# Gathers behind a branch, loads behind a gather, an earlier w_in, and a new set of aims in a fused attention, expert and MLP kernel

## The chip, the cores and the metric

The kernel runs on one core of one Trainium2 chip. The metric is the device time of one execution in microseconds (us), lower is better. The engines are PE (matmul), DVE (VectorE), ACT (ScalarE), POOL (GpSimd) and SP, which issues most transfers; POOL issues the indirect ones. Each engine takes its instructions in order.

## The reference

Three stages follow each other. x is [4, 576, 512].

```python
# 1: attention, 4 batches x 8 heads, seq 576, head_dim 64
scores = q @ k.T / sqrt(64)
keep = scores >= max(scores) - tau            # tau = 0.02, the rest is masked out
x = softmax(scores where keep) @ v            # heads side by side: [4, 576, 512]

# 2: one of 8 experts for each token, with a sticky choice along the sequence
logits = x @ w_gate;  gate = sigmoid(x @ w_local)
e[s] = argmax(logits[s]) if s == 0 or gate[s] < 0.5 else e[s-1]
x = softmax(logits)[e] * (relu(x @ w1[e]) @ w2[e])       # w1: 512x1024, w2: 1024x512

# 3: gated MLP over tokens
h = gelu_tanh(x @ w_in);  u, v = h[:512], h[512:]
vn = layernorm(v) * g_ln
out = x + (u * (w_sg @ vn + b_sg)) @ w_out               # w_sg mixes the 576 positions
```

## The kernel before

**One list.** Every operation of the kernel is put into one graph with an engine, a planned duration and an aim (a due time), and a list scheduler turns it into five queues, one per engine. `Graph.order` picks by aim, and the operations run in the order that it chose. The recorded operations are issued from one helper, so in the profile most of the later stages carry the line L183. Attention's aims come from `Attn.build` with tables (`OFFS`, `PER` and the letters in `KE`, `QE`, `KL`, `QL`, `NB`), the later ones from `Tail.P` and `PRIO`. An aim decides only the place in a queue; the hardware waits by semaphores.

**Attention.** 144 row tiles (128 rows x 576 columns) go through scores (L427), row maximum on DVE (L432), the negated maximum (`nb`: ACT L440 or POOL L442), exponential on ACT (L447), mask and sum on DVE (L456), transposes (L476) and the product with v (L515, L517). Each of the 32 head and batch pairs has its q and k split into a high part (rounded copy, on ACT L380 or DVE L382) and a low part (the remainder, L395 for k and L406 for q, on DVE or POOL). The letters of the tables name the engine for each: A, D or P.

**Routing.** `Route` works in two halves of the tokens and a rest. A half is some thirty small operations on DVE and a few on PE. Half A ends in L1123 on DVE and L1128 on PE; it says which expert is first (`oe`), so that its weights can be loaded and its first two tiles gathered before attention is over. The rest gives the permutation `inv` for all tokens (rank counts, L1210 on PE), from which every tile of 128 tokens is gathered out of `x_dram` by POOL.

**Experts.** 22 tiles in the order of the experts, with the capacities CAPS = (5, 3, 3, 3, 2, 2, 2, 2). The first expert's first two tiles run in `plain` in full float32; its other three, and all tiles of the experts 1 to 7, run as three products of high and low parts. The weights of an expert are eight loads of 512 KB (`wld`), taken into a ring of six buffers (c_75 to c_80), split by ACT (high) and DVE (low). Expert 0 is followed by a branch (`over`, L1697) for tiles that overflow the capacities; it isn't taken here, but every engine reads a register and jumps at that place. The aim of the branch is `more` in `Tail.P`.

```python
g.gather(need - a * P["gth"], gth, w=[xg], deps=dep["A"] if t < 2 else dep["R"], name="gth")   # L1386
W8.append(split(*load(i, k, need, st, [dep["rank"]]), need, self.WLO[i]))                      # L1479
```

**Conversions and MLP.** Beside the experts' work twelve conversions (`cv`: three steps on DVE, three on POOL, one on DVE) rewrite `w_in` and `w_out` into `wi` and `wo` in device memory. The MLP takes its rows in groups of three tiles. Its four slices of `w_in` are loaded from `wi` into the same ring and split: high parts on ACT, low parts (`two`, 128x1024) in turn on POOL and DVE. The first group's tiles are gathered by POOL from `ys`, where the experts stored their rows; PE holds 30 bf16 matmuls without a use (`idle`) ahead of the first transposes.

## Time and profile before

| what | us |
|---|---|
| median of three runs (797.89 to 801.44) | 799.79 |
| the profiled execution | 798.59 |
| its span | 796.8 |
| PE busy in it | 764.4 |
| DVE busy in it | 580.7 |
| ACT busy in it | 461.6 |
| POOL busy in it | 268.5 |

The profile is one execution. The span is the time from its first to its last instruction; 1.8 us of the execution lie outside it. PE's busy time is that of its matmuls, and idle time is put down to the operation whose end came last before PE went on. "PEq" there is PE's own sequencer, and "issue" is time in which the profile shows nothing that was waited for. The mean granted clock of PE is 0.998 of full speed over the execution.

### The profile page before, as it was taken

How to read it: one execution, taken by the hardware profiler on the slowest of the kernel's cores; microseconds unless marked ns; L12 is line 12 of the kernel's file. 1: busy time of each engine (PE TensorE's matmuls, PEld its weight loads, DVE VectorE, ACT ScalarE, POOL GpSimd, SP SyncE). 2: the span in 40 equal slices, each digit the busy share in tenths (PEclk: the TensorE clock that was granted, in tenths of full speed). 3: DMA queues.
4: the chain of work that ended last, by engine and by line, in shares of the span. 5: the costliest groups of instructions: out<-in, count | busy, mean ns of one | idle time of the engine just before them, and what ended most of it. 6: DMA issues, size and time to landing. Idle time of an engine off the chain costs nothing.

```text
span 796.8 us, 13834 instructions
## 1 busy us (share of the span) xinstructions
PE 764.4 (96%) x4832; PEld 653.0 (82%) x4832; DVE 580.7 (73%) x1226; ACT 461.6 (58%) x860; POOL 268.5 (34%) x411
## 2 busy tenths in 40 slices
PE   7999999999979999799999999999999999999997
PEld 4787788888857876488898889989788999899996
DVE  7998999999999966465766667774379743587632
ACT  6888788889868864263444345543386532366410
POOL 6335143333333100312544232253675233111410
PEclk9999999999999999999999999999999999999999
DMA  7342323453253024768485576754440012300012
GB/s 211 101 151 74 110 86 126 157 175 124 61 197 117 2 80 146 227 225 278 163 275 203 179 247 223 236 194 159 146 142 0 1 53 93 84 11 1 14 41 66
DMA packets 46912, 103.18 MB, mean 129 GB/s; under 512 B 7538, under 2 KB 7538, under 8 KB 46834
## 3 DMA queue, kind: packets, MB, share of 16 engines
q1 hardware_dynamic: 43634, 91.72, 34.9%
q0 software_dynamic: 3200, 10.49, 4.5%
q8 instruction: 40, 0.66, 0.3%
q14 instruction: 38, 0.31, 0.1%
HBM read 80.17 MB, written 22.02 MB: 128 GB/s over the span
## 4 chain that ended last, share of the span: by engine, by line
PE 48%; DVE 4%; POOL 2%; DMA 2%; issue 1%; ACT 1%; SPq 0%; POOLq 0%; DVEq 0%; ACTq 0%
PE PS L183 48%; DVE MF L183 2%; POOL MF L183 1%; DVE r L183 1%; POOL r L183 1%; DMA MF<-in_w_in_dram 1%; DMA wi<-MF 1%; DMA MF<-ys,MF 1%; ACT MF L183 1%; DVE bs L183 0%; ACT r L183 0%; DVE rq L183 0%; SPq L183 0%; DVE mv L183 0%; PE PS L1251 0%
## 5 line engine op out<-in xcount | busy, mean ns | idle before, releaser
L183 PE MATMUL PS<-r,r 128*128 128x512 f32 (+3 forms) x1512 | 294.2, 352 | 2.2 <-DVE r L183 1.6
L183 PEld LDWEIGHTS PS<-r,r 128*128 128x128 f32 x1512 | 254.9, 189 | 34.1 <-DVE r L183 3.4
L427 PE MATMUL PS<-MR 128*128 128x288 f32 x640 | 122.2, 319 | 7.9 <-DVE MF L456 6.0
L456 DVE SCALAR_TENSOR_TENSOR MF<-PS,MF 128x576 f32<-128x576 f32 x144 | 116.2, 810 | 8.2 <-ACT MF L447 5.6
L447 ACT ACTIVATE MF<-PS,MF 128x576 f32<-128x576 f32 x144 | 107.0, 749 | 10.6 <-DVE MF L432 9.2
L432 DVE TENSOR_REDUCE MF<-PS 128x1 f32<-128x576 f32 x144 | 106.6, 751 | 7.2 <-PE PS L427 6.2
L427 PEld LDWEIGHTS PS<-MR 128*128 128x128 f32 x640 | 91.6, 189 | 17.3 <-DVE MF L456 10.3
L183 PE MATMUL PS<-MR,r 128*128 128x256 f32 (+2 forms) x616 | 101.7, 322 | 0.0
L183 ACT ACTIVATE r<-PS 128x512 fp32r<-128x512 f32 (+4 forms) x102 | 46.3, 472 | 94.5 <-PE PS L183 89.0
L183 PEld LDWEIGHTS PS<-MR,r 128*128 128x128 f32 x616 | 91.6, 188 | 8.1
L369 ACT ACTIVATE c<-PS 128x512 f32<-128x512 f32 (+1 forms) x160 | 84.7, 566 | 20.5 <-PE PS L476 15.2
L476 PE MATMUL PS<-ident,MF 128*128 128x128 f32 x576 | 84.2, 275 | 3.3 <-ACT c L503 1.9
L476 PEld LDWEIGHTS PS<-ident,MF 128*128 128x128 f32 x576 | 67.3, 140 | 8.1 <-ACT c L369 3.0
L183 ACT ACTIVATE MF<-PS 128x512 f32<-128x512 f32 (+1 forms) x64 | 35.6, 555 | 65.9 <-PE PS L183 50.9
L442 POOL TENSOR_TENSOR MF<-MF,cf 128x1 f32<-128x1 f32 x104 | 23.3, 225 | 138.7 <-DVE MF L432 110.6
L183 DVE TENSOR_TENSOR r<-c,r 128x1024 fp32r<-128x1024 f32 x42 | 52.0, 1265 | 22.3 <-ACT r L183 21.9
L183 DVE SCALAR_TENSOR_TENSOR MF<-MF,PS 128x384 f32<-128x384 f32 (+1 forms) x84 | 49.9, 606 | 20.8 <-ACT MF L183 20.0
L183 DVE SCALAR_TENSOR_TENSOR r<-PS,r 128x384 fp32r<-128x384 f32 (+3 forms) x64 | 29.1, 455 | 47.4 <-ACT r L183 47.3
L183 POOL TENSOR_SCALAR MF<-MF 128x512 f32<-128x512 int32 x12 | 21.9, 1825 | 102.6 <-DVE MF L183 62.1
L183 ACT ACTIVATE r<-c 128x1024 fp32r<-128x1024 f32 x46 | 46.8, 1056 | 11.1 <-PE PS L183 5.8
L183 PE MATMUL PS<-r,MR 128*128 128x320 f32 (+2 forms) x288 | 44.6, 315 | 5.4 <-PEq L1697 4.1
L183 PEld LDWEIGHTS PS<-r,MR 128*128 128x128 f32 x288 | 43.5, 195 | 6.6 <-DVEq L1697 4.3
(233 smaller groups left out, 1053.1 us busy)
## 6 DMA issues: line engine op xcount, KB each, us to landing
c<-in_w_dram SPq DMA_DIRECT2D x64, 512.0 KB, 4.5
c<-in_kP_dram SPq DMA_DIRECT2D x32, 288.0 KB, 3.5
c<-in_qP_dram SPq DMA_DIRECT2D x32, 288.0 KB, 3.1
ys<-MF SPq DMA_DIRECT2D x36, 256.0 KB, 4.3
x_dram<-c SPq DMA_DIRECT2D x6, 768.0 KB
MF<-in_w_in_dram SPq DMA_DIRECT2D x8, 512.0 KB
c<-in_vP_dram SPq DMA_DIRECT2D x12, 320.0 KB, 5.4
out_dram<-MF SPq DMA_DIRECT2D x12, 256.0 KB, 2.0
```

Of the source, the lines that this page charges most:

```text
L183: return lambda *a, **k: x(*[v(y) for y in a], **{n: v(y) for n, y in k.items()})
L369: self.nc.scalar.activation(out, src, AF.Copy, **k)
L427: self.nc.tensor.matmul(self.PS[:, banks[hf], 0:288], q, k[:, 288 * hf:288 * hf + 288], start=(n == 0), stop=(n == len(ops) - 1))
L432: self.nc.vector.tensor_reduce(m, self.tl[i]["s"], axis=AX.XY, op=ALU.min)
L442: (self.nc.vector if eng == "DVE" else self.nc.gpsimd).tensor_tensor(self.nbt(i), self.tl[i]["m"], self.tp, op=ALU.add)
L447: self.nc.scalar.activation(e.rearrange("p (a b) -> p a b", a=2), t["s"], AF.Exp, bias=t["m"], scale=-1.0)
L456: self.nc.vector.scalar_tensor_tensor(w.rearrange("p (a b) -> p a b", a=2), t["s"], self.nbt(i), t["e"].rearrange("p (a b) -> p a b", a=2) ...
L476: self.nc.tensor.transpose(p[:, c, :], t["w"][:, z + c * 128:z + (c + 1) * 128], self.cst["ident"])
```

## The change

**Dependences.** Gathers of the tiles from CAPS[0] = 5 on, which belong to the experts 1 to 7, now depend on the branch (`g.more`). A new transfer of four bytes, `hold0`, reads tile 4 after its gather and writes it into a scrap word; all loads of weights of the experts 1 to 7 depend on it. The transposes of the MLP's second group for tile i wait for the matmuls `vp` of tile i of the first.

**w_in.** Its loads are aimed 16 us earlier (T - 26 in place of T - 10), its splits 14 us earlier, and all four low parts are on DVE; POOL had two of them.

**Tables.** In attention three low parts of k (`KL` places 26, 27, 31) and two of q (`QL` 17, 30) go from DVE to POOL; of the high parts one of k (`KE` 4) and three of q (`QE` 19, 23, 31) go from ACT to DVE and one of q (`QE` 15) from DVE to ACT. Of 18 tiles five gave their negated maximum to ACT and now three do, which is 16 of 144 more on POOL. `OFFS`, `PER`, `PRIO` and `Tail.P` are new.

```diff
--- before.py
+++ after.py
@@ -238,19 +238,19 @@
     XALL, X2T, RR, EP, WP, Z, SM, LOG = 24576, F, F + 1152, F + 1736, F + 2888, F + 6920, F + 8072, F + 8200
 
 
-    KE = "AAAAAAADAAADDADAAADADAAADAAAAAAA"
-    QE = "DADAAAAAAADAADADADAAADAAAAAAAAAA"
-    KL = "PPPPDPPDPDPPPPPDDPPPPPPPPPDDDPPD"
-    NB = "PAAPAPAAPPPPPPPPPP"
-    QL = "DPPDPPPPPPPPDPPPPDPPPPDDPPPPPPDP"
-    PER = 1.8433
+    KE = "AAAADAADAAADDADAAADADAAADAAAAAAA"
+    QE = "DADAAAAAAADAADAAADADADADAAAAAAAD"
+    KL = "PPPPDPPDPDPPPPPDDPPPPPPPPPPPDPPP"
+    NB = "PAPPPPPPPPPPPAAPPP"
+    QL = "DPPDPPPPPPPPDPPPPPPPPPDDPPPPPPPP"
+    PER = 1.8091
     WB = 6
     ALPHA = 0.05368
     side = ()
     extra = ()
     WARM = (9, 2, 2, 2, 2)
     WARMP = 0.0
-    OFFS = dict(c=3.643, rem=1.219, mx=-1.591, qk=-5.409, x2t=0.022, remx=-4.025, nb=-5.597, nbm=6.508, ex=-3.128, prep=-0.874, mask=0.758, av=7.252, tr=4.058, rec=2.530, ld=-39.498, post=9.454, qd=53.614)
+    OFFS = dict(c=3.372, rem=1.016, mx=-1.496, qk=-4.928, x2t=4.442, remx=-3.519, nb=-6.117, nbm=0.077, ex=-3.520, prep=-1.662, mask=1.432, av=6.737, tr=4.551, rec=2.717, ld=-36.254, post=9.490, qd=55.875)
 
 
     SEQ = [(n, t) for t in range(9) for n in range(2)]
@@ -1277,7 +1277,7 @@
     ALPHA = (0.0326, 0.03152)
     PA = 14.8
     W0, W1 = 14.8, 23.1
-    P = dict(more=1.886, wld=13.828, whi=-5.404, wlo=6.969, gth=35.799, cv=45.362, xT=18.099, s=23.033, mgth=17.296, sgl=-14.414, fin=7.434, vh=63.286, sg=26.995, wo=46.385)
+    P = dict(more=-12.300, wld=19.348, whi=-5.770, wlo=11.562, gth=36.897, cv=31.147, xT=12.357, s=25.298, mgth=16.824, sgl=-12.676, fin=9.956, vh=63.991, sg=25.660, wo=50.081)
     WLO = "DDDDDDDD"
 
     WR = tuple(33792 + 1024 * i for i in (0, 1, 2, 3, 5, 4))
@@ -1362,7 +1362,7 @@
             a = self.ALPHA[0]
             g.op("ACT", act(1024), need - a * P["whi"], lambda: nc.scalar.activation(h, raw, AF.Copy), r=[wr], w=[uh], name="whi")
             if lo == "D":
-                g.op("DVE", dve(1024), need - a * P["wlo"], lambda: nc.vector.tensor_tensor(l, raw, h.bitcast(F32), op=ALU.subtract), r=[wr, uh], w=[ul], name="wlo")
+                g.op("DVE", 1.35, need - a * P["wlo"], lambda: nc.vector.tensor_tensor(l, raw, h.bitcast(F32), op=ALU.subtract), r=[wr, uh], w=[ul], name="wlo")
             else:
                 g.op("POOL", pool(1024), need - a * P["wlo"], lambda: nc.gpsimd.tensor_tensor(l, raw, h.bitcast(F32), op=ALU.subtract), r=[wr, uh], w=[ul], name="wlo")
             return [uh, ul], h, l
@@ -1383,7 +1383,10 @@
                     nc.tensor.transpose(p.ap[:, k * 128:(k + 1) * 128], x[:, k * 128:(k + 1) * 128], ident)
 
             q = lambda: p.ap.rearrange("p (a b) -> p a b", a=4)[:, :, 0:n]
-            g.gather(need - a * P["gth"], gth, w=[xg], deps=dep["A"] if t < 2 else dep["R"], name="gth")
+            g.gather(need - a * P["gth"], gth, w=[xg], deps=dep["A"] if t < 2 else dep["R"] + ([g.more] if t >= CAPS[0] else []), name="gth")
+            if t == CAPS[0] - 1:
+
+                self.hold0 = g.op("DQ", 0.1, need - a * P["gth"], lambda: nc.sync.dma_start(out=self.scrap[0:1, 1:2], in_=x[0:1, 0:1]), r=[xg], name="hold")
             g.op("PE", 0.44, need - a * P["xT"], tr, r=[xg], pw=p, deps=deps, name="xT")
             g.op("ACT", act(512, True), need - a * 2, lambda: nc.scalar.activation(xh, q(), AF.Copy), w=[xt], pr=p, name="xh")
             if xl is not None:
@@ -1476,7 +1479,7 @@
                 W8 = []
                 for i in range(8):
                     need = W(T + 0.3 * i if i < 4 else T + L1 + 1.3 * (i - 4))
-                    W8.append(split(*load(i, k, need, st, [dep["rank"]]), need, self.WLO[i]))
+                    W8.append(split(*load(i, k, need, st, [dep["rank"], self.hold0]), need, self.WLO[i]))
             hh, hl = self.M(self.HH, [128, 8, pitch], F32R), self.M(self.HL, [128, 8, pitch], F32R)
             hu = [g.use((self.HH + pitch * m, pitch), (self.HL + pitch * m, pitch)) for m in range(8)]
             if k == 0:
@@ -1569,7 +1572,7 @@
         def two(parts, n, h, l, raw, wr, t, eng, rows=slice(0, 128)):
             u = g.use(*parts)
             g.op("ACT", act(n), t, lambda: nc.scalar.activation(h[rows], raw[rows, 0:n], AF.Copy), r=[wr], w=[u], name="shi")
-            e, d = (nc.vector, dve(n)) if eng == "DVE" else (nc.gpsimd, pool(n))
+            e, d = (nc.vector, 1.35) if eng == "DVE" else (nc.gpsimd, pool(n))
             g.op(eng, d, t, lambda: e.tensor_tensor(l[rows], raw[rows, 0:n], h[rows].bitcast(F32), op=ALU.subtract), r=[wr, u], w=[u], name="slo")
             return u
 
@@ -1582,8 +1585,8 @@
         for k in range(4):
             wr = R["wr"].new()
             raw = self.wr[wr.i]
-            g.op("DQ", 1.46, W(T - 10), lambda k=k, raw=raw: nc.sync.dma_start(out=raw, in_=w_in[k * 128:(k + 1) * 128, :]), w=[wr], deps=self.conv, name="sld")
-            self.wiu.append(two([(s[0] + 2048 * k, 2048)], 1024, self.wi[0][:, k, :], self.wi[1][:, k, :], raw, wr, W(T - 2), "DVE" if k % 2 else "POOL"))
+            g.op("DQ", 1.46, W(T - 26), lambda k=k, raw=raw: nc.sync.dma_start(out=raw, in_=w_in[k * 128:(k + 1) * 128, :]), w=[wr], deps=self.conv, name="sld")
+            self.wiu.append(two([(s[0] + 2048 * k, 2048)], 1024, self.wi[0][:, k, :], self.wi[1][:, k, :], raw, wr, W(T - 16), "DVE"))
         self.two, self.V = two, V
 
     def s_weights2(self, after):
@@ -1754,7 +1757,7 @@
         st = [dict(x2={}, v={}, u={}) for _ in range(2)]
         ones = g.op("POOL", 2.7, W(self.P["sg"]), self.v_rows, w=[g.use(*[(x, 512) for k in (8, 9) for x in A["v"][k]])], name="rows")
 
-        first = []
+        first, self.vp = [], []
 
         def gelu2(pb, n, dst, du, t):
 
@@ -1812,10 +1815,10 @@
                     o = g.op("DVE", 0.4, W(need - 4), lambda t=t, x=x: v.tensor_scalar(x, x, self.pg[p][:, t:t + 1], None, op0=ALU.mult), r=[xu], w=[xu], name="xpg")
                     if i == 2:
 
-                        self.hold = g.op("DQ", 0.1, W(need - 4), lambda x=x: nc.sync.dma_start(out=self.scrap, in_=x[0:1, 0:1]), r=[xu], name="hold")
+                        self.hold = g.op("DQ", 0.1, W(need - 4), lambda x=x: nc.sync.dma_start(out=self.scrap[0:1, 0:1], in_=x[0:1, 0:1]), r=[xu], name="hold")
                 else:
                     g.op("ACT", act(512), W(need - 4), lambda t=t, x=x: nc.scalar.activation(x, x, AF.Copy, scale=self.pg[p][:, t:t + 1]), r=[xu], w=[xu], deps=first, name="xpg")
-                g.op("PE", 0.43, W(need - 3), tr, r=[xu], deps=self.busy if p == gi == 0 else (), pw=pb, name="xT")
+                g.op("PE", 0.43, W(need - 3), tr, r=[xu], deps=self.busy if p == gi == 0 else self.vp[i:i + 1] if p == 0 and gi == 1 else (), pw=pb, name="xT")
                 g.op("ACT", act(512, True), W(need - 2.5), lambda c=c, q=q: nc.scalar.activation(self.x2h[:, :, c], q(), AF.Copy), w=[xt[i]], pr=pb, name="xh")
                 o = g.op("DVE", dve(512), W(need - 2), lambda c=c, q=q: v.tensor_tensor(self.x2l[:, :, c], q(), self.x2h[:, :, c].bitcast(F32), op=ALU.subtract), r=[xt[i]], w=[xt[i]], pr=pb, name="xl")
             if p == gi == 0:
@@ -1833,7 +1836,7 @@
                         for n, (a, b) in enumerate(((self.x2h, 0), (self.x2h, 1), (self.x2l, 0))):
                             nc.tensor.matmul(pb.ap, a[:, k, c], self.wi[b][:, k, 512:1024], start=(k == 0 and n == 0), stop=(k == 3 and n == 2))
 
-                g.op("PE", pe(512, 12), W(T[0]), mm, r=[xt[i]] + self.wiu, pw=pb, name="vp")
+                self.vp.append(g.op("PE", pe(512, 12), W(T[0]), mm, r=[xt[i]] + self.wiu, pw=pb, name="vp"))
                 T[0] += pe(512, 12)
                 v2u, bsu = R["v2"].new(), R["bs"].new()
                 v2, bs = self.v2[v2u.i], self.bs[bsu.i]
@@ -1969,7 +1972,7 @@
     STEPS = (("G", 0, 0), ("G", 0, 1), ("G", 0, 2), ("g", 0, 0), ("g", 0, 1), ("G", 1, 0), ("G", 1, 1), ("G", 1, 2), ("g", 1, 0), ("g", 1, 1), ("4", 1, 0))
 
 
-PRIO = (10.5, 8.806, 9.0)
+PRIO = (12.465, 7.256, 9.256)
 
 
 @with_exitstack
@@ -1993,7 +1996,7 @@
     x_dram = tc.dram_tile([T, D], F32, name="x_dram")
     ys = tc.dram_tile([(NT + NOV) * 128, D], F32, name="ys")
     wi32 = tc.dram_tile([D, 2 * D], F32, name="wi32")
-    scrap = tc.dram_tile([1, 1], F32, name="scrap")
+    scrap = tc.dram_tile([1, 2], F32, name="scrap")
     wo32 = tc.dram_tile([D, D], F32, name="wo32")
     nc = tc.nc
 

```

What the tables do to the queues is not to be read from the diff. Three places follow.

**The end of attention on SP.** In these rows c_72 and c_73 take q and k, c_75 to c_78 the first expert's first four loads, and x_dram is the store of attention's result. Before, on SP, with attention's last two pairs of k and q behind the first expert's loads:

```order
L183 DMA c_75<-in_w_dram 128x1024
...
L183 DMA c_76<-in_w_dram 128x1024
...
L183 DMA c_77<-in_w_dram 128x1024
...
L183 DMA c_78<-in_w_dram 128x1024
L347 DMA c_72<-in_kP_dram 128x576
...
L343 DMA c_72<-in_qP_dram 128x576
L347 DMA c_73<-in_kP_dram 128x576
...
L343 DMA c_73<-in_qP_dram 128x576
L567 DMA x_dram<-c_74 128x3x512 x3
```

In the changed program the same stretch of SP reads:

```order
L347 DMA c_72<-in_kP_dram 128x576
...
L343 DMA c_72<-in_qP_dram 128x576
L347 DMA c_73<-in_kP_dram 128x576
...
L343 DMA c_73<-in_qP_dram 128x576
...
L183 DMA c_75<-in_w_dram 128x1024
...
L183 DMA c_76<-in_w_dram 128x1024
...
L183 DMA c_77<-in_w_dram 128x1024
...
L183 DMA c_78<-in_w_dram 128x1024
L567 DMA x_dram<-c_74 128x3x512 x3
```

The first expert's loads moved behind all of attention's loads; they wait for half A of the routing, which moved with them.

**The branch on SP and POOL.** Here c_75 to c_80 take weights of expert 1, ys are stores of the first expert's rows, scrap is `hold0`, and x_dram with inv_91 are gathers of the tiles from 2 on (inv_92 are those inside the branch). SP ahead of the branch before:

```order
L183 DMA c_78<-in_w_dram 128x1024
L183 ISA
L183 DMA c_80<-in_w_dram 128x1024
L183 ISA
L183 DMA c_79<-in_w_dram 128x1024
L183 DMA ys<-MF 128x512
L183 ISA
L183 DMA c_75<-in_w_dram 128x1024
L183 DMA ys<-MF 128x512
L183 TENSOR_LOAD oi
L183 ISA x2
L1697 COMPARE_AND_BRANCH
```

SP ahead of the branch in the changed program:

```order
L183 DMA c_76<-in_w_dram 128x2x512
L183 DMA scrap<-MF 1x1
L183 DMA MF<-in_g_ln_dram 128x512
L183 TENSOR_LOAD op
...
L183 DMA c_78<-in_w_dram 128x1024
L183 DMA ys<-MF 128x512
...
L183 DMA c_80<-in_w_dram 128x1024
L183 DMA ys<-MF 128x512
L183 TENSOR_LOAD oi
...
L1700 COMPARE_AND_BRANCH
```

Of the four loads of expert 1 two moved behind the branch, and the other two stand behind `hold0` and the load of gln. POOL around the branch before, its body left out:

```order
L183 MEMSET r_3147 128x8x64 x2
L183 DMA MF<-x_dram,inv_91 128x512 x7
L183 TENSOR_LOAD oi
L1697 COMPARE_AND_BRANCH
...
L1697 UNCONDITIONAL_BRANCH
L183 DMA MF<-x_dram,inv_91 128x512 x4
```

POOL around the branch in the changed program, its body left out:

```order
L183 MEMSET r_3142 128x8x64 x2
L183 DMA MF<-x_dram,inv_91 128x512 x3
L183 TENSOR_LOAD oi
L1700 COMPARE_AND_BRANCH
...
L1700 UNCONDITIONAL_BRANCH
L183 DMA MF<-x_dram,inv_91 128x512 x8
```

Of the seven gathers ahead of the branch three are left, and eight stand directly behind it where four stood.

**The entry of the MLP on POOL and DVE.** Here r_3110 and r_3104 are the buffers of the split weights, c_75 to c_79 the loaded slices of w_in, and ys the experts' stored rows. POOL up to the first gathers of the MLP, before:

```order
L183 TENSOR_TENSOR MF<-MF 128x512 x2
L183 MEMSET r_3110 64x512
L183 MEMSET r_3110 1x512 x2
L183 MEMSET r_3110 64x512
L183 MEMSET r_3110 1x512 x2
L183 TENSOR_TENSOR r_3110<-c_79,r_3110 128x1024
L183 TENSOR_TENSOR r_3110<-c_76,r_3110 128x1024
L183 DMA MF<-ys,MF 128x512 x7
```

POOL up to the same gathers in the changed program:

```order
L183 TENSOR_TENSOR MF<-MF 128x512 x2
L183 MEMSET r_3104 64x512
L183 MEMSET r_3104 1x512 x2
L183 MEMSET r_3104 64x512
L183 MEMSET r_3104 1x512 x2
L183 DMA MF<-ys,MF 128x512 x7
```

The two low parts in front of POOL's gathers are gone. DVE there before (128x192 are evacuations of the last expert's first layer, MF 128x512 alone steps of conversions and, as the last, of the MLP's entry):

```order
L183 SCALAR_TENSOR_TENSOR r_3147<-PS,r_3147 128x192 x2
L183 SCALAR_TENSOR_TENSOR MF<-MF 128x512
L183 SCALAR_TENSOR_TENSOR r_3147<-PS,r_3147 128x192 x6
L183 TENSOR_TENSOR r_3110<-c_75,r_3110 128x1024
L183 TENSOR_TENSOR r_3110<-c_77,r_3110 128x1024
L183 TENSOR_SCALAR MF<-MF 128x512 x3
L183 TENSOR_TENSOR r_3147<-PS,r_3147 128x4x128 x3
```

DVE at the same place in the changed program:

```order
L183 SCALAR_TENSOR_TENSOR r_3142<-PS,r_3142 128x192
L183 SCALAR_TENSOR_TENSOR MF<-MF 128x512
L183 SCALAR_TENSOR_TENSOR r_3142<-PS,r_3142 128x192 x6
L183 TENSOR_TENSOR r_3104<-c_79,r_3104 128x1024
L183 SCALAR_TENSOR_TENSOR r_3142<-PS,r_3142 128x192
L183 TENSOR_TENSOR r_3104<-c_75,r_3104 128x1024
L183 TENSOR_TENSOR r_3104<-c_76,r_3104 128x1024
L183 TENSOR_TENSOR r_3104<-c_77,r_3104 128x1024
L183 TENSOR_SCALAR MF<-MF 128x512 x3
```

Four low parts stand where two did, the first of them ahead of the last evacuation of the last expert's first layer.

## Rows read from the trace of the kernel before

**Rows 1.** Page, part 1: busy us (share of the span) of each engine.

```profile
PE 764.4 (96%) x4832; PEld 653.0 (82%) x4832; DVE 580.7 (73%) x1226; ACT 461.6 (58%) x860; POOL 268.5 (34%) x411
```

**Rows 2.** PE's waits over the span: us in total, times, longest.

```profile
PE PS L427 <- DVE MF L456: 6.0, 10, 1.3
PE PS L183 <- DVE r L183: 3.0, 3, 1.5
PE PS L1128 <- DVE MF L1123: 2.3, 1, 2.3
```

**Rows 3.** Stretches: length, busy PE, PEld, DVE, ACT, POOL; clock, DMA share, GB/s.

```profile
100.00:200.00 100.00, 99.73 (x751) 82.33 (x750) 94.62 (x207) 86.23 (x173) 36.65 (x68) 1.00 0.41 133
220.00:240.00 20.00, 15.49 (x121) 11.88 (x118) 19.38 (x59) 13.19 (x25) 7.96 (x10) 1.00 0.64 215
260.00:280.00 20.00, 20.00 (x156) 16.84 (x157) 18.11 (x39) 17.49 (x36) 2.76 (x11) 1.00 0.01 2
280.00:300.00 20.00, 19.18 (x132) 14.70 (x129) 12.72 (x25) 12.91 (x25) 1.90 (x5) 1.00 0.21 79
```

**Rows 4.** Lines L395, L440, L442: duration ns min/median/max, starts.

```profile
L395 POOL TENSOR_TENSOR MR<-c,MR x24: 1393/1414/1525, 13.3 to 258.8; 64x576 fp32r<-64x576 f32 x24
L395 DVE TENSOR_TENSOR MR<-c,MR x6: 743/756/907, 18.9 to 250.4; 64x576 fp32r<-64x576 f32 x6
L440 ACT ACTIVATE MF<-MF,cf x40: 283/295/333, 10.7 to 268.2; 128x1 f32<-128x1 f32 x40
L442 POOL TENSOR_TENSOR MF<-MF,cf x104: 180/190/758, 9.2 to 287.5; 128x1 f32<-128x1 f32 x104
```

**Rows 5.** PE's timeline, first expert and jump: start, length, operation [idle before].

```profile
326.81 1.23 PE L183 MATMUL PS<-ident,MF 128*128 128x128 f32 x8 [1.87 <-DVE MF L1143]
339.50 12.34 PE L183 MATMUL PS<-r,MR 128*128 128x320 f32 x72 [4.08 <-PEq L1697]
```

**Rows 6.** Gathers and loads by timeline, and issues of 318 to 342 with landing.

```profile
320.45 7.35 SPq L183 DMA_DIRECT2D c<-in_w_dram  x3
320.96 1.33 POOL L183 DMA_INDIRECT MF<-x_dram,inv  x1 [14.76 <-DVE MF L1228]
MF<-x_dram,inv POOLq DMA_INDIRECT x8, 5.1
565.27 1.03 POOL L183 DMA_INDIRECT MF<-ys,MF  x1 [0.15 <-issue]
568.69 0.49 DVE L183 TENSOR_SCALAR MF<-MF 128x512 f32<-128x512 f32 x1 [5.84 <-DMA MF<-ys,MF]
```

**Rows 7.** The jump: line L1697 by engine; its DMA queue; one stretch.

```profile
L1697 PEldq COMPARE_BRANCH  x1: 6043/6043/6043, 333.3 to 333.3; - x1
L1697 DVEq COMPARE_BRANCH  x1: 72/72/72, 335.1 to 335.1; - x1
L1697 DVEq EVENT_SEMAPHORE  x1: 21/21/21, 339.0 to 339.0; - x1
q14 instruction: 7, 0.06, 0.8%
336.00:338.00 2.00, 0.00 (x0) 0.00 (x0) 0.00 (x0) 0.00 (x0) 0.00 (x0) 1.00 0.34 120
```

**Rows 8.** Clock behind the jump, by stretch (columns as in rows 3).

```profile
341.00:342.00 1.00, 1.00 (x5) 1.00 (x5) 0.00 (x0) 0.00 (x0) 0.00 (x0) 0.50 0.83 82
340.00:360.00 20.00, 20.00 (x116) 18.35 (x115) 14.62 (x27) 11.79 (x17) 3.50 (x4) 0.91 0.73 236
```

**Rows 9.** Entry of the MLP: POOL's and DVE's timeline, PE's waits 566 to 610.

```profile
558.73 6.38 POOL L183 TENSOR_TENSOR r<-c,r 128x1024 fp32r<-128x1024 f32 x2
558.28 1.22 DVE L183 TENSOR_TENSOR r<-c,r 128x1024 fp32r<-128x1024 f32 x1 [1.54 <-ACT r L183]
560.17 2.68 DVE L183 TENSOR_TENSOR r<-c,r 128x1024 fp32r<-128x1024 f32 x1 [0.67 <-ACT r L183]
PE PS L183 <- issue: 1.9, 2, 1.5
```

## The prediction

> **What bounds the kernel now.** I read the busy shares first: TensorE (PE) is busy 764.4 of 796.8 us and no other engine is above 581 [rows 1]. So the time is PE's work plus what PE idles, and nothing here changes PE's work: the same matmuls stand in the changed program, in another order. Therefore I went to PE's waits, which say what each idle stretch ended on [rows 2], to the busy time by stretch, which says where another engine is as full as PE [rows 3], and then to the timelines around the three places that the diff moves things: first gathers, branch, entry of the MLP [rows 5 to 9]. The reader is to see that the attention stage is bound by PE and nearly as much by VectorE (DVE: PE 99.73, DVE 94.62 of 100 us), that the largest single idle stretch of PE is the jump over the overflow branch, 4.08 us, and that behind it PE runs for a while at half clock.
>
> The sum is made against the profiled execution: 798.59 us, span 796.8. The median of the three runs is 799.79, 1.2 above it, so 1.2 is added at the end.
>
> **1. Gathers of tiles 5 and later behind the branch, loads of experts 1 to 7 behind tile 4's gather.** Today PE runs out of the first expert's matmuls and waits 1.87 us until 326.81; the transposes there need a gathered tile [rows 5]. That gather was issued at 320.96, beside three loads of expert 1, 512 KB each, that SP issued in the 7.35 us from 320.45 on, so it took up to 5.9 us; the eight gathers of that stretch take 5.1 us in the median [rows 6]. The nearest row of a gather without such loads is the one at the MLP's entry: issued at 565.27, its reader starts at 568.69, 3.4 us later [rows 6]. In the changed order the loads wait for tile 4, and ahead of the first transpose PE has the same four matmuls and the same second group of rank counts as before. A gather that is 2.4 us shorter more than covers a wait of 1.87. I take **-1.9 us**, bounds -1.9 and 0 (the time stays 5.1 or more for a reason of its own). What becomes late instead are loads of expert 1: six of eight issue after the branch, where SP resumes at about 340. At the 236 GB/s of 340 to 360 [rows 8] the two that complete its first matrix, and eight gathers of 256 KB, are 3.1 MB or 13 us, over by about 353; expert 0's rest runs on PE until well after that (72 matmuls of its first layer take 12.34 us from 339.50 on [rows 5], and its second layer follows). So nothing is taken for that, at most +2. The wait of SP for the tiny transfer `hold0` holds back gln, two loads and two stores, which nobody needs there before the branch.
>
> **2. The branch.** PE idles 4.08 us, until 339.50 [rows 5], so its last matmul in front ends at 335.4. PE's sequencer had reached the jump at 333.3 and spent 6.04 us in it; DVE reached it at 335.1 and was through at 339.0, 3.9 us later [rows 7]. PE came 1.8 us before DVE and left at nearly the same time, so what let them go was common to both. Code for the engines came by DMA in this stretch (seven packets on q14 alone), and it shares the DMA engines with the data, which took 0.34 of their time even from 336 to 338 [rows 7]; today four gathers and two loads more stand in front than in the changed program. If each jump takes DVE's 3.9 us, PE, whose sequencer is 2.1 us ahead of its matmuls, idles 1.8; if it is still the whole 6.04, it idles 4.1 as now. I take 2.0, that is **-2.1 us**, near to the shortest row because fewer transfers stand in front; bounds -4.1 (no wait at all) and +1 (POOL and SP reach the jump later than now, since both wait for gathers).
>
> **3. The clock behind it.** The granted clock is 0.50 from 341 to 342 and 0.91 in the mean of 340 to 360 [rows 8]; these are 1.2 GHz and a mean with 2.4: 20 x 0.09 = 1.8 us of work lost. It fell after the idle of 4.08 us; after the 2.3 us that PE idled for L1123 [rows 2] it did not (mean clock 1.00 in 220 to 240 [rows 3]). With an idle of 2.0 the second row is the nearer one: **-1.8 us**, bounds -1.8 and 0.
>
> **4. w_in.** The two low parts that leave POOL held it for 6.38 us from 558.73, in front of the gathers [rows 9]; the first gather went at 565.27 [rows 6]. They also wait for the last expert's stored tiles, which come at the end of its second layer, so they can't go earlier by the 6.38. At the entry PE waits 1.9 us in two pieces that no engine's work explains [rows 9]; the first transpose there is covered by 30 idle matmuls. Of the 1.9 I take about a third, **-0.7 us**, bounds -1.9 and +1.2. The upper bound is a low part of 1.22 us [rows 9]: the first of the four now stands on DVE ahead of the last expert's eighth evacuation.
> Of the two low parts that DVE has today one took 1.22 us; the other, wholly beside POOL's, took 2.68 [rows 9]. Four on DVE are 4.9 us by the first row and 10.7 by the second; DVE has the room while the last expert's second layer runs, so the sum stays. The Trainium skill (GPSIMD Engine Reference, 8. Key points) says that POOL shares its SBUF interfaces with VectorE, and that VectorE's instructions with two SBUF inputs, as these are, contend with it. The 2.68 agrees. By that rule the move would pay twice at the entry, where POOL has no low part left, and cost up to 1.46 us a piece where POOL still converts beside it.
>
> **5. Attention tables.** DVE loses five low parts of 0.756 us and gains three high copies of about 0.5: -2.2 us. POOL gains five of 1.414 and 16 negations of 0.190 and ACT loses those of 0.295 [rows 4]: nothing on a full engine. The routing of half A moves from 225 to about 260 us; there PE waits 2.3 us for it (L1128 for L1123 [rows 2]) and 4.51 in 220 to 240 in all, since DVE is full (19.38 of 20). From 260 to 300 DVE has 1.89 + 7.28 = 9.2 us free [rows 3]. So the follow-up idle of 4.5 - 2.3 = 2.2 us may go, the 2.3 will stay (the block is still one piece on DVE). Half of 2.2: **-1.0 us**; bounds -4.5 (the whole idle of 220 to 240) and +4.5 (the block costs as much again in the lighter stretch, since the tables aimed wrong). The first expert's weights come some 35 us later, in a stretch in which the DMA engines stand at 0.01 [rows 3]: nothing.
>
> **6. Experts.** The conversions stand elsewhere on DVE. Today PE waits 3.0 us in three places for DVE's evacuation behind such a conversion [rows 2]. The new order still has conversions in front of evacuations: **0**, bounds -3.0 and +5.4.
>
> Sum: -1.9 - 2.1 - 1.8 - 0.7 - 1.0 + 0 = -7.5, so 798.59 - 7.5 = 791.1, and 1.2 on top: **792.3 us**.
>
> **Rivals.**
> A. The jump costs what it costs. The transfers in front are not what it waits for. For it: from 336 to 338 the DMA engines were at 0.34 only, and DVE still stood until 339.0 [rows 7]. Then 2 and 3 are nothing: -3.6, 792.3 + 3.9 = 796.2, and with an idle longer by the bound of +1, 797.2; I name 797.
> The Trainium skill (Runtime: NRT & Kernel Launch, Instruction fetch mechanics) states that a taken branch to a page that is not resident forces a DMA fetch before execution goes on. By that rule alone the stall is the fetch's own time and moved gathers would give nothing in 2 and 3; no row here shows a jump with idle DMA engines.
> B. Slower: POOL's queue in attention. 16 more tiles send their negated maximum through POOL, where they can stand behind a low part of 1.414 us; the exponential and the mask on DVE wait for it. A full wait costs 1.414 + 0.190 - 0.295 = 1.3 us, all 16 cost 20.9. To end slower by over 0.5% it takes 11.5 us, so nine of them: 804; with twelve 808. Against it: 104 negations go that way today [rows 4], and PE's waits for masks are 6.0 us in all [rows 2]. I name 805.
> C. Attention pays more: where DVE has room, the block no longer empties PE's queue: -4.5 in place of -1.0, 788.8.
> D. The conversions in the experts collide anew: six pairs each expose 1.4 us, about what the larger two of today's three waits do, 8.4 - 3.0 = +5.4: 797.7.
>
> **How the numbers follow.** About 0.5% of 799.8, 4.0 us, is what a measurement of this kernel can tell from no change: the borders are 795.8 and 803.8. Forecast 0.48 (own range 788.5 to 797; 0.42 of it below 795.8), A 0.18, B 0.13, C 0.10, D 0.11. Faster 0.42 + 0.10 = 0.52; same 0.06 + 0.18 + 0.11 = 0.35; slower 0.13. The range 788 to 801 leaves out B and a little of C.
>
> **What would show it.** Step 1: no wait of PE between the second rank counts and the first transposes, and gathers of some 3.5 us. Step 2: PE idle at the jump near 2 us, DVE's jump at or below 3.9. Step 3: clock 1.00 behind it. Step 4: the waits of 1.9 us at the MLP's entry near 1. Step 5: PE's wait for L1123 stays near 2.3, at about 260, with less idle after it. It is wrong if PE idles 4 us or more at the jump, if L427's wait for masks rises above 6.0 us, or if evacuations in the experts cost more than 3.0.

## The result, and the profile after

The changed kernel takes 793.02 us in the median of seven runs (790.36 to 796.37), the kernel before 799.79 (797.89 to 802.63). The ratio is 0.9906, 95% interval 0.9884 to 0.9927: 6.8 us or 0.9% faster. (It is taken over all runs, so it isn't quite that of the two medians.) The forecast was 792.3. Its total held, but nearly every term of its sum did not, so the experiments ask where the 6.8 us really came from.

The profiled execution took 792.77 us with a span of 790.7. Its page answers [rows 1] with the same work on PE and a little more on POOL:

```profile
PE 762.9 (96%) x4831; PEld 653.2 (83%) x4832; DVE 583.8 (74%) x1226; ACT 457.4 (58%) x841; POOL 274.2 (35%) x430
```

PE's waits over the span (us in total, times, longest), against [rows 2]:

```profile
PE PS L427 <- DVE MF L456: 4.0, 6, 1.3
PE PS L183 <- PEq L1700: 3.9, 1, 3.9
PE PS L183 <- DVE r L183: 2.5, 4, 1.1
PE PS L183 <- DMA MF<-x_dram,inv: 0.9, 1, 0.9
```

The wait for L1123 is gone, that for masks fell from 6.0 to 4.0, and that for evacuations (DVE taking PE's results out of its accumulators) from 3.0 to 2.5. The jump (L1700 now) still costs 3.9. By stretch, against [rows 3] (length, busy PE, PEld, DVE, ACT, POOL; clock, DMA share, GB/s):

```profile
220.00:240.00 20.00, 19.83 (x150) 16.73 (x149) 18.04 (x40) 16.98 (x35) 6.68 (x13) 1.00 0.38 123
260.00:280.00 20.00, 18.26 (x147) 14.66 (x146) 18.84 (x64) 13.95 (x28) 3.93 (x11) 1.00 0.34 133
280.00:300.00 20.00, 20.00 (x126) 15.56 (x123) 12.83 (x30) 12.12 (x25) 3.18 (x4) 1.00 0.42 145
```

PE works 19.83 of the 20 us from 220 on, where it had 15.49; where the routing of half A stands now it loses 1.74. PE's timeline, against [rows 5] (start, length, operation, idle before and what ended it):

```profile
263.23 0.59 PE L1128 MATMUL PS<-MF 128*128 128x2 bf16 x18
```

```profile
320.76 0.66 PE L183 MATMUL PS<-ident,MF 128*128 128x128 f32 x4 [0.90 <-DMA MF<-x_dram,inv]
332.28 12.34 PE L183 MATMUL PS<-r,MR 128*128 128x320 f32 x72 [3.90 <-PEq L1700]
```

L1128 follows without idle. One gather is still waited for, 0.90 us. PE restarts behind the jump at 332.28, where it did at 339.50: 7.2 us earlier. From there to the end it takes 790.7 - 332.28 = 458.4 us, where it took 457.3. So all of the gain was made ahead of the jump, and 1.1 us were lost behind it.

Around the jump, against [rows 7], first the line's instructions (duration ns min/median/max, start us), then two stretches:

```profile
L1700 PEldq COMPARE_BRANCH  x1: 5903/5903/5903, 326.2 to 326.2; - x1
L1700 DVEq COMPARE_BRANCH  x1: 72/72/72, 328.0 to 328.0; - x1
L1700 DVEq EVENT_SEMAPHORE  x1: 21/21/21, 332.4 to 332.4; - x1
```

```profile
326.00:328.00 2.00, 2.00 (x16) 2.00 (x15) 0.49 (x1) 0.44 (x1) 0.00 (x0) 1.00 0.99 304
328.00:330.00 2.00, 0.38 (x3) 0.11 (x1) 0.00 (x0) 0.00 (x0) 0.00 (x0) 1.00 0.77 300
```

PE spends 5.90 us in the jump (6.04 before), and the DMA engines are as full beside it as they were, 0.99 and then 0.77. SP's timeline says with what:

```profile
322.52 0.34 SPq L183 DMA_DIRECT2D c<-in_w_dram  x1
324.38 0.34 SPq L183 DMA_DIRECT2D c<-in_w_dram  x1
```

These are two loads of expert 1, held back until tile 4 was there. In `e1_attn` below, which has no such wait, SP issued four loads of expert 1 from 312.96 to 320.90. Of the four, two are now behind the branch and these two run beside the jump. The load of gln (256 KB) came forward as well, to 321.10; it stood behind the jump before (340.47). Last, POOL at the entry of the MLP, against [rows 6, 9], and PE's waits there:

```profile
556.87 1.03 POOL L183 DMA_INDIRECT MF<-ys,MF  x1 [6.36 <-issue]
```

```profile
PE PS L183 <- issue: 2.2, 2, 1.5
```

POOL has been free for 6.36 us before its first gather, so here the gathers wait for something else. The gather comes 2.81 us after SP issued the store in front of it (554.06), where it came 3.07 us after it before (562.20): the low parts on POOL had held it up by no more than about 0.3 us. The four low parts on DVE take 1.22 us each in the mean, with no low part beside them on POOL. In `e8_nowin`, where POOL has its two again, DVE's two take 5.55 us together.

### The profile page after: what moved, and what is told of

It reads as the page before. It is cut to its first block, busy times and chain, and to the rows that moved or that the text cites. A ratio compares the mean times of both kernels' runs of the same rounds, so it can differ in the third digit from the quotient of the medians.

```text
span 790.7 us, 13848 instructions
## 1 busy us (share of the span) xinstructions
PE 762.9 (96%) x4831; PEld 653.2 (83%) x4832; DVE 583.8 (74%) x1226; ACT 457.4 (58%) x841; POOL 274.2 (35%) x430
## 4 chain that ended last, share of the span: by engine, by line
PE 47%; DVE 5%; DMA 2%; issue 2%; POOL 1%; ACT 1%; POOLq 0%; DVEq 0%; SPq 0%; ACTq 0%
PE PS L183 47%; DVE r L183 2%; DVE MF L183 2%; POOL MF L183 1%; DMA wi<-MF 1%; DMA MF<-ys,MF 1%; DVE bs L183 0%; DMA c<-in_w_dram 0%; ACT MF L183 0%; ACT r L183 0%; DMA out_dram<-MF 0%; DVE rq L183 0%; DVE mv L183 0%; PE PS L1251 0%; DVE rqi L183 0%
## 5 line engine op out<-in xcount | busy, mean ns | idle before, releaser
L427 PE MATMUL PS<-MR 128*128 128x288 f32 x640 | 122.6, 321 | 7.0 <-DVE MF L456 4.0
L427 PEld LDWEIGHTS PS<-MR 128*128 128x128 f32 x640 | 92.5, 190 | 15.1 <-DVE MF L456 7.7
L442 POOL TENSOR_TENSOR MF<-MF,cf 128x1 f32<-128x1 f32 x120 | 27.7, 232 | 138.5 <-DVE MF L432 125.5
L183 DVE TENSOR_TENSOR r<-c,r 128x1024 fp32r<-128x1024 f32 x44 | 58.2, 1341 | 12.3 <-ACT r L183 11.6
L183 POOL TENSOR_SCALAR MF<-MF 128x512 f32<-128x512 int32 x12 | 19.2, 1599 | 98.3 <-DVE MF L183 60.4
L183 POOL DMA_INDIRECT MF<-x_dram,inv x22 | 28.1, 1278 | 59.0 <-PE PS L183 28.0
```

The lines of the kernel that those rows point to most:

```text
L183: return lambda *a, **k: x(*[v(y) for y in a], **{n: v(y) for n, y in k.items()})
L427: self.nc.tensor.matmul(self.PS[:, banks[hf], 0:288], q, k[:, 288 * hf:288 * hf + 288], start=(n == 0), stop=(n == len(ops) - 1))
L442: (self.nc.vector if eng == "DVE" else self.nc.gpsimd).tensor_tensor(self.nbt(i), self.tl[i]["m"], self.tp, op=ALU.add)
```

## The experiments

Times are medians of four to ten runs, and ratios are to runs of the kernel before on the same chip (medians 799.99 to 800.67 us). My theory after the result: the gain is attention's, and the dependences, whose gain I had forecast, give nothing because they move traffic to the jump. The rival is the forecast's own reasoning: gathers and jump.

### One half of the change at a time

`e1_attn`: the kernel before with attention's tables (KE, QE, KL, NB, QL, PER and OFFS, all as in the change) and the routing's aims.

```diff
-    KE = "AAAAAAADAAADDADAAADADAAADAAAAAAA"
+    KE = "AAAADAADAAADDADAAADADAAADAAAAAAA"
 ...
-    OFFS = dict(c=3.643, rem=1.219, ...
+    OFFS = dict(c=3.372, rem=1.016, ...
 ...
-PRIO = (10.5, 8.806, 9.0)
+PRIO = (12.465, 7.256, 9.256)
```

> The kernel before with attention's new tables and routing aims alone; no gather or load is made to wait, w_in and the tail's aims are as before. Theory 1 (most of the gain was made before the first expert's rank counts, in attention): about 794, 6 us under before, PE restarting behind the jump about 6 us earlier than before's 339.5, and no wait of PE for L1123. Rival (the gain is that of the gathers and of the jump): 798.5 or more, at most 1.3 us under before.

`e2_rest`: the changed kernel with the reverse of that diff, so all the rest of the change.

```diff
-    KE = "AAAADAADAAADDADAAADADAAADAAAAAAA"
+    KE = "AAAAAAADAAADDADAAADADAAADAAAAAAA"
 ...
-PRIO = (12.465, 7.256, 9.256)
+PRIO = (10.5, 8.806, 9.0)
```

> The changed kernel with attention's tables and the routing aims of before: gathers behind the branch, hold0, w_in and the tail's aims stay. Theory 1: 798.5 to 800, that is at most 1 us from the first transposes' wait (1.87 becomes about 0.9) and nothing from the jump; PE waits 2.3 us for L1123 again. Rival: 793 to 795.

Measured: `e1_attn` 790.16 us, ratio 0.9898 (0.9853 to 0.9944); `e2_rest` 799.86, ratio 1.0005 (0.9982 to 1.0028). Attention's half is worth at least as much as the whole change (its median is 2.9 us lower than the changed kernel's, but the two ratios, 0.9898 and 0.9906, lie well within each other's intervals), and the other half nothing by itself. `e1_attn` came out 4 us below what I had expected. Its trace shows why: the jump is short there (PE's waits, then PE's timeline):

```profile
PE PS L183 <- PEq L1697: 1.8, 1, 1.8
```

```profile
331.64 10.80 PE L183 MATMUL PS<-r,MR 128*128 128x320 f32 x72 [1.78 <-PEq L1697]
```

PE idles 1.78 us in place of 4.08, and the 72 matmuls behind it take 10.80 us in place of 12.34 [rows 5], since the clock doesn't fall. `e1_attn` has no dependence of the change, its last load in front of the jump was issued at 320.90, and the DMA engines are at 0.31 beside the jump.

### The dependences and w_in alone

`e3_nodeps`: the changed kernel without them.

```diff
-deps=dep["A"] if t < 2 else dep["R"] + ([g.more] if t >= CAPS[0] else [])
+deps=dep["A"] if t < 2 else dep["R"]
-split(*load(i, k, need, st, [dep["rank"], self.hold0]), need, self.WLO[i])
+split(*load(i, k, need, st, [dep["rank"]]), need, self.WLO[i])
```

> The changed kernel without the new dependences: gathers of tiles 5 and later are free again, loads of expert 1 don't wait for hold0. Theory 1: about 794, 1 us over the changed kernel: the wait ahead of the first transposes returns to 1.5 to 2 us, the jump stays at 3.9 to 4.1. Rival (the dependences carry the gain): 797 or more.

Measured: 791.47 us, 0.9905 (0.9881 to 0.993). That is no slower than the changed kernel, against both theories' numbers. The gathers' waits returned as expected (2.5 us in two places), but the jump fell to 1.8 us and paid for them. So in these traces the dependences gain 1.6 us at the gathers and lose 2.1 at the jump and 1.5 to the half clock behind it (72 matmuls in 10.80 and 12.34 us). In the medians that is nothing that the spread of the runs lets one tell from zero.

`e8_nowin`: the changed kernel with w_in loaded and split as before.

```diff
-W(T - 26) ... W(T - 16), "DVE"
+W(T - 10) ... W(T - 2), "DVE" if k % 2 else "POOL"
```

> The changed kernel with the old loads and splits of w_in, two low parts on POOL again. Theory 1 (the MLP's entry waits for the stored tiles and the gathers, not for POOL): within 0.7 us of the changed kernel, waits at the entry 2 to 3 us in sum as there. Rival (the low parts on POOL hold the gathers up): 1 to 2 us slower than the changed kernel, first gather 1 us or more later behind its store.

Measured: 793.58 us, 0.993 (0.9912 to 0.9947). Within 0.7 us of the changed kernel, as theory 1 said, and a difference that the spread of the runs covers.

### What the jump waits for

`e4_quiet`: the changed kernel with the loads of the experts 1 to 7, those of the conversions and gln behind the branch.

```diff
-split(*load(i, k, need, st, [dep["rank"], self.hold0]), need, self.WLO[i])
+split(*load(i, k, need, st, [dep["rank"], self.hold0, g.more]), need, self.WLO[i])
-w=[gu], deps=[dep["slot"]], name="gln"
+w=[gu], deps=[dep["slot"], g.more], name="gln"
-w=[u], deps=self.dep["R"], name="cvl"
+w=[u], deps=self.dep["R"] + [g.more], name="cvl"
```

> The changed kernel with all loads of weights of the experts 1 to 7, the conversions' loads and gln behind the branch as well, so that only two stores of rows stand on SP in front of the jump. Theory 2 (the jump lasts as long as data transfers run beside it, and the loads that hold0 held back run beside it now): PE idles 1.8 us at the jump in place of 3.9, no half clock behind it, about 0.9 us ahead of the transposes: 789.5 to 790.5. Rival A (the jump has its own length): 3.9 and 793. Rival (expert 1's weights come too late): a new wait of PE for DVE or a load between 340 and 370, and 793 or more.

Measured: 790.9 us, 0.9898 (0.9858 to 0.9937). PE's wait at the jump:

```profile
PE PS L183 <- PEq L1700: 1.5, 1, 1.5
```

1.5 us, no half clock, and 0.9 us for the gather as in the changed kernel. The 72 matmuls behind the jump start at 329.79 and take 10.80 us, so they end 4.0 us earlier than in the changed kernel, and the profiled span is 4.3 us shorter (786.4 against 790.7). The medians differ by 2.1 us only, with four runs from 788.46 to 792.96 against seven from 790.36 to 796.37. The traces show the jump's part, and the medians agree in direction.

`e10_bquiet`: the same three edits in the kernel before, without `hold0`.

```diff
-split(*load(i, k, need, st, [dep["rank"]]), need, self.WLO[i])
+split(*load(i, k, need, st, [dep["rank"], g.more]), need, self.WLO[i])
 ...
```

> The kernel before with the same three kinds of loads behind the branch; its seven gathers in front of the jump stay, and so does attention. Theory 2: jump 4.08 to 1.8, no half clock, and the first transposes wait less than 1.87, because no load runs beside the gathers: 800 - 2.3 - 1.5 - 0.9 to 1.9 = 794.3 to 795.3. Rival A: only the gathers' wait goes, 798 to 799.

Measured: 797.51 us, 0.9972 (0.9948 to 0.9996). The jump costs PE 2.3 us and the gathers 0.8, both in the direction of theory 2, but the total fell by 2.8 and not by 5 to 6. The clock fell behind the jump all the same, for 3.4 us from 338.6 on, as long as in the kernel before. And in the profiled execution it fell a second time, for 3.4 us from 226 on, where PE had waited 2.3 us for L1123; the profiled execution of the kernel before shows no fall there.

`e5_short`: the changed kernel, transfers untouched, with a short body of the branch.

```diff
             tsplit(x, xh, xl)
+            chunk(0)
+            if k >= 0:
+                return
 ...
-            for k in range(2):
-                tile(k)
-            with tc.If(number > 2):
-                for k in range(2, NOV):
-                    tile(k)
+            tile(0)
```

> The changed kernel with the body of the branch, which isn't executed, cut to the start of one tile (PE 379 instructions fewer to jump over). Loads and gathers stay as in the changed kernel. Theory 2a (what waits in the jump is the fetch of code that lies far behind it, and data transfers delay that fetch): with the near target PE idles under 1 us, no half clock, 788.5 to 790. Rival (the jump waits for something else that the transfers hold, not for code): PE idles 3.9 us as in the changed kernel, 793.

Measured: 787.63 us, 0.9835 (0.9801 to 0.9869), the lowest median of all, level with `e6_nobranch` below. The jump by engine, the stretch beside it, and PE's timeline:

```profile
L1703 PEldq COMPARE_BRANCH  x1: 236/236/236, 326.3 to 326.3; - x1
L1703 DVEq COMPARE_BRANCH  x1: 72/72/72, 327.7 to 327.7; - x1
L1703 DVEq EVENT_SEMAPHORE  x1: 21/21/21, 327.9 to 327.9; - x1
```

```profile
326.30:329.30 3.00, 2.85 (x20) 2.62 (x19) 0.98 (x2) 0.88 (x2) 0.71 (x1) 1.00 0.98 311
```

```profile
324.14 15.03 PE L183 MATMUL PS<-r,MR 128*128 128x320 f32 x96
```

PE passes the jump in 0.24 us and runs 96 matmuls in one piece, with the DMA engines at 0.98. So it is not traffic as such that holds the jump. The queues that bring code show what is missing (packets, MB, share, 318 to 333 us), first in the changed kernel, then here:

```profile
q8 instruction: 2, 0.03, 0.8%
q14 instruction: 5, 0.04, 0.8%
```

```profile
q8 instruction: 1, 0.02, 0.5%
```

The five packets on q14 all run while PE stands in the jump (328.5 to 332.0); with the near target q14 brings none. So what PE waits for is the fetch of code that lies far behind the jump, and `e4_quiet` shows that traffic delays it: same code, fewer transfers, 3.52 us in place of 5.90.

`e6_nobranch`: the changed kernel without the branch.

```diff
-        number = nc.values_load(oi[0:1, NOV:NOV + 1], min_val=0, max_val=NOV)
-        with tc.If(number > 0):
-            for k in range(2):
-                tile(k)
-            with tc.If(number > 2):
-                for k in range(2, NOV):
-                    tile(k)
```

> The changed kernel with no branch at all (the tiles of overflow, of which there are none here, have no code). It prices the jump: 3.9 us of idle and 1.5 us of half clock less give 787.6; where the work behind the jump isn't ready any earlier, the wait turns into one for a gather or a load, and 789 to 791 come out.

Measured: 787.7 us, 0.9838 (0.9805 to 0.987): the jump's whole price in the changed kernel is 5.3 us by the medians, and `e5_short` takes it all away.

The time that PE spends in the jump, and the DMA engines' share in the 3 us after PE reached it, in thirteen traces:

| kernel | DMA share | PE in the jump, us | PE idle, us |
|---|---|---|---|
| before | 1.03 | 6.04 | 4.1 |
| changed | 0.97 | 5.90 | 3.9 |
| e8_nowin | 0.96 | 5.80 | 3.8 |
| e11_bprio | 0.79 | 5.68 | 3.7 |
| e2_rest | 0.79 | 4.70 | 3.7 |
| e10_bquiet | 0.73 | 4.24 | 2.3 |
| e13_tables | 0.40 | 4.22 | 2.2 |
| e14_best | 0.31 | 3.90 | 1.9 |
| e3_nodeps | 0.31 | 3.80 | 1.8 |
| e1_attn | 0.31 | 3.74 | 1.8 |
| e4_quiet | 0.30 | 3.52 | 1.5 |
| e12_letters | 0.29 | 3.54 | 1.6 |
| e5_short | 0.98 | 0.24 | 0 |

A far jump is some 3.5 us beside little traffic and 6 beside full traffic. In between the share alone doesn't order the rows: at 0.73 to 0.79 the jump takes 4.2 to 5.7 us. (In `e2_rest` the profile puts PE's idle time down to an evacuation on DVE, which came out of its own jump at 340.3.) The Trainium skill (Runtime: NRT & Kernel Launch, Instruction fetch mechanics) says that a taken branch out of the resident pages forces a DMA fetch of its target. The last line agrees with it: with the near target there is no stall.

### Inside attention

`e11_bprio`: the kernel before with the new PRIO alone.

```diff
-PRIO = (10.5, 8.806, 9.0)
+PRIO = (12.465, 7.256, 9.256)
```

> The kernel before with the routing's three aims alone (half A later). Theory 3 (the place of half A is what attention's gain rests on): no wait for L1123, idle of 220 to 300 us from 6.3 to about 3.5, 795 to 796.5. Rival (the tables make it): 798.5 to 800.

`e13_tables`: the kernel before with attention's tables alone, so the first diff of this section without PRIO.

```diff
-    KE = "AAAAAAADAAADDADAAADADAAADAAAAAAA"
+    KE = "AAAADAADAAADDADAAADADAAADAAAAAAA"
 ...
-    OFFS = dict(c=3.643, rem=1.219, ...
+    OFFS = dict(c=3.372, rem=1.016, ...
```

> The kernel before with attention's letters, period and aims alone, the routing's aims as before, so that half A stays near 225 us. Theory 3: the wait for L1123 stays at 2 to 2.5 us, idle of 20 to 100 falls by about 1 as in the changed kernel, 797.5 to 799. Rival (the tables make it): 793 to 795.

`e12_letters`: the same without the new OFFS.

```diff
-    OFFS = dict(c=3.372, rem=1.016, ...
+    OFFS = dict(c=3.643, rem=1.219, ...
```

> The kernel before with attention's letters (which engine does which part) and its period alone; the twelve aims of attention and those of the routing are as before. Theory (the letters carry the 6.0 us of attention's tables, because DVE loses 2.2 us and ACT 6.9 us of work where both are nearly full): 794.5 to 796. Rival (the aims carry it): 798 to 800.

Measured: `e11_bprio` 798.49 (0.9981, 0.9957 to 1.0005), `e13_tables` 794.31 (0.9924, 0.9904 to 0.9944), `e12_letters` 795.91 (0.9947, 0.9927 to 0.9968). Theory 3 falls: the later place of half A alone gives little, and the wait for L1123 moves with it. The tables came out in their rival's range, and the letters in their theory's, but with a jump of 1.6 us that this theory hadn't counted. The wait in `e11_bprio`, then in `e13_tables`:

```profile
PE PS L1128 <- DVE MF L1123: 2.0, 1, 2.0
```

```profile
PE PS L1128 <- DVE MF L1123: 1.3, 1, 1.3
```

With both it is gone. Medians mix this with the jump, which is short in `e13_tables` and `e12_letters`. Attention alone is seen where PE starts the 24 matmuls ahead of the jump, less the waits for gathers: 329.5 in the kernel before, 330.0 in `e11_bprio`, 328.3 in `e13_tables`, 328.8 in `e12_letters`, 323.3 in `e1_attn`, 323.4 in the changed kernel. The three in the middle ran 6.8 us at half clock on the way (0.83 from 260 to 280 in `e11_bprio`, 0.83 from 220 to 240 in the other two). By PE's busy time in it that is 2.5 to 2.7 us of lost work, an upper bound, since PE also waited there. The kernel before and `e1_attn` lost nothing, the changed kernel 1.7 us in its first 20. As they stand, tables give 1.2 us, the routing's aims -0.5, and both 6.2. With all of the lost work given back it is 3.9, 2.0 and 6.2. So both together beat either alone, but how much they do beyond their sum isn't resolved. The traces show where it lands, in the idle of 220 to 300: 6.3 us before, 5.0 and 4.3 with one of them, 3.1 with both. There DVE makes no mask for 8.4 us around the routing's block (from 255.4 to 263.8 in the changed kernel), and PE doesn't wait for L1123. That it has more queued there is the likely reason; no run isolates it.

### A version built from both findings

`e14_best`: the kernel before with attention's tables and the routing's aims, gathers from tile 5 on and the loads of `e10_bquiet` behind the branch, no `hold0`; w_in and the tail's aims as before.

```diff
-deps=dep["A"] if t < 2 else dep["R"], name="gth")
+deps=dep["A"] if t < 2 else dep["R"] + ([g.more] if t >= CAPS[0] else []), name="gth")
-split(*load(i, k, need, st, [dep["rank"]]), need, self.WLO[i])
+split(*load(i, k, need, st, [dep["rank"], g.more]), need, self.WLO[i])
 ...
-PRIO = (10.5, 8.806, 9.0)
+PRIO = (12.465, 7.256, 9.256)
```

> The kernel before with attention's tables and the routing's aims, and with gathers of tiles 5 and later, all loads of the experts 1 to 7, the conversions' loads and gln behind the branch; no hold0, w_in and the tail's aims as before. If the three findings so far add up (attention, quiet gathers, quiet jump): 790.2 for attention alone less 1.5 for the gathers' waits, the jump as short as there: 788 to 789. If the late loads cost a wait behind the jump, 790 or more.

Measured: 789.56 us, 0.9865 (0.9829 to 0.9901): 3.5 us under the changed kernel's median and 10 to 11 under the kernel before. That is just above the 788 to 789 expected: the 1.5 us of the gathers did not add to `e1_attn`, whose median is 0.6 us away, within the runs' spread. Against the changed kernel the intervals of the two ratios still overlap. In its trace the gather's wait is 0.9 us and the jump's 1.9, but this time the clock fell behind the jump (0.91 in 320 to 340). `e5_short` has a lower median still, but its branch can't serve overflow.

## Why the prediction was right in its sum and wrong in its steps

**1, gathers (-1.9): half right.** The wait fell from 1.87 to 0.90. The first tile came in time, as forecast; the third did not. I had asked only for the first. The third gather was issued at 315.98, held POOL for 2.01 us, and its transposes start at 320.76. That is 4.8 us later, where I took 3.4, with no load of weights beside it but behind two other gathers: loads were only part of what made a gather long.

**2, jump (-2.1): failed, -0.2.** The mechanism was the one named, with traffic that delays the fetch of code: `e4_quiet` got 1.5 us idle. Only the reading that one thing lets all engines go is not borne out: there PE leaves at 329.7, ACT at 330.0 and DVE at 330.7. The step that failed is "fewer transfers stand in front". I counted transfers in SP's queue and didn't ask when they would run. `hold0` took the loads out of 313 to 321 and put two of them, and gln, into 321 to 329, right onto the jump. Rival A (797) had the changed kernel's own jump right and its reason wrong.

**3, clock (-1.8): failed in the profiled run.** With 3.9 us of idle the clock fell again: 72 matmuls take 12.34 us as before. Nor was the forecast's own idle of 2.0 us safe. In the profiled executions the clock held behind idle times of 1.5 to 1.8 us at the jump (10.80 us in `e1_attn`, `e3_nodeps`, `e4_quiet`, `e12_letters`), and fell behind 1.9 (`e14_best`), 2.2 (`e13_tables`) and 2.3 (`e10_bquiet`). The row it was taken from, 2.3 us at L1123 without a fall, was one execution.

**4, entry of the MLP (-0.7): failed.** The wait there rose from 1.9 to 2.2 us, with 0.6 more for DVE. POOL was not the bound; `e8_nowin` gives the same time within its spread. That the stored rows and the gathers are the bound is argued, not tested. The price of a low part was right: 1.22 us each without POOL's beside it. But the row of 1.22 was no clean one, since POOL's ran beside 0.8 us of it.

**5, attention (-1.0): the term that was mis-sized.** It measured about -6. I took the half-A wait as fixed ("the 2.3 will stay"), since the block is one piece on DVE, and it went to zero where it stands now, as `e1_attn` shows too. I had also counted only idle. Up to the restart behind the jump PE's busy time fell by 1.9 us as well (317.68 to 315.78). Why isn't shown: the matmuls of L427, the largest group, take as long as before (319 and 321 ns in the mean). The bound of -4.5 was too near, too.

**6, experts (0): about right.** Waits for evacuations between the jump and the MLP fell from 2.8 to 1.4 us; what was lost behind the jump, 1.1 us in all, lies in the MLP, and there not at its entry. From the restart behind the jump to the 72 matmuls that follow the first transposes both kernels take 234.52 us. The rest comes later, with a new wait of 0.98 us for DVE at 714.76, and its cause stays open.

B (POOL's queue) did not show: the wait for masks fell to 4.0. C was the rival nearest to what happened. That the number held is luck: the gain in attention was 5 us larger than forecast, and gathers, jump, clock and entry together gave 5 to 6 us less. None of the three signs of being wrong came up, though the jump's 3.9 us missed its 4 by little.

## What to carry over

Ask of a transfer that is made to wait not only who no longer shares the wire with it, but what it will run beside then; beside full traffic a far jump took some 2 us more, and a short body behind the branch removes the question. When two halves of a change can be built apart, build them apart: here one half carried everything and the other gave nothing that the runs can show. Forecast a table of aims with at least the whole idle of the stretch it touches as the bound, and not by half of what looks movable; here even the whole of it, 4.5 us, was less than the gain.

## What the runs showed of the hardware

The granted clock also fell after shorter idle than the 4 us of the jump. In `e13_tables` it was 0.83 in the mean of 220 to 240: 1.00 up to 228.6, then half until 235.5. PE had waited 1.3 us for L1123 and stood in a wait of 1.9 us for a mask when it fell:

```profile
220.00:240.00 20.00, 16.39 (x118) 13.25 (x115) 16.15 (x63) 10.70 (x19) 5.65 (x12) 0.83 0.63 226
```

The kernel before had a longer wait there, 2.3 us, and no fall in its profiled run; `e10_bquiet` and `e2_rest`, with the same tables of attention, did fall there. So it isn't the same in each execution, and part of the spread of the runs goes with it: of 60 runs of the kernel before, the 26 with a mean clock of 0.991 or less take 801.0 us in the median, the 12 with 0.996 or more 798.5. The seven runs of the changed kernel go from 790.36 at 1.000 to 796.37 at 0.992. The mean clock is 0.9924 over those 60 runs and 0.9956 over the seven, so the profiled run of before, at 0.998, hid part of what its other runs lose. The gain in clock goes with attention's half: the mean is 0.9924 in the ten runs of `e2_rest` and 0.996 in the four of `e1_attn`. A part of the gain in the medians is thus a clock that fell less often, which the forecast counted only behind the jump; 0.003 of 790 us would be some 2.5 us, an estimate from these means.
